# A second level of seven products inside products 1 and 4 of the up layer, three of four pairs of groups, in a routing attention followed by a squared-ReLU layer

## The chip, the core and the metric

The kernel runs on one core of a Trainium2 chip. The core has a matrix engine (TensorE, PE in the profile; its weight loads are PEld), a vector engine (VectorE, DVE), an engine for activation functions (ScalarE, ACT), a general engine (GpSimd, POOL) and one that mostly issues transfers (SyncE, SP). Each runs its own instructions in order and waits for the others on semaphores. Matmuls write to PSUM[...]; all else lies in SBUF, 128 partitions wide. The metric is the time of one execution on the device in microseconds; less is better.

## The reference

```python
def _attn_ref(q, k, v, centroids):            # B, H, S, D = 4, 8, 768, 64; 16 centroids
    q_assign = np.argmax(np.einsum('bhsd,hcd->bhsc', q_n, c_n), axis=-1)
    k_assign = np.argmax(np.einsum('bhsd,hcd->bhsc', k_n, c_n), axis=-1)
    mask = q_assign[:, :, :, None] == k_assign[:, :, None, :]
    scores = scale * np.matmul(q, k.transpose(0, 1, 3, 2))
    scores = np.where(mask, scores, -1000000000.0)
...
    return np.matmul(attn, v).astype(np.float32)

def _moe_ref(x, w_in, w_out):                 # x 3072x512, w_in 512x2048, w_out 2048x512
    h = x @ w_in
    r = np.maximum(h, 0.0)
    g = r * r
    return (g @ w_out).astype(np.float32)
```

The attention's output, turned to 3072 rows of 512, is the x of the second part. The change touches only `h = x @ w_in` and the square.

## The kernel before

**Stages.** The attention runs first, up to about 320 us. Then the four batches follow each other in the order of FEED, 1, 2, 3, 0; each has an up stage (h and its square) and a down stage (times w_out). The first batch (n = 0) has code of its own, `first_up` and `first_down`. The others (n = 1, 2, 3) run `up` and then `Down.run`. Everything from n = 1 on has its order written out by hand: an engine runs its instructions in the order in which the program issues them.

**An up stage.** All matrices are stored with the contracted dimension on the partitions. w_in is 4 x 128 rows by 2048 columns, x of a batch 4 x 128 rows by 768 columns. Each up stage splits all three matrices in two by two and uses Strassen's scheme with seven products in place of eight (the variant of Winograd). The loop `for i in range(F2)` goes over eight groups; a group makes four blocks of 128 x 384: c11 and c12 (row block i, the two halves of the columns) and c21 and c22 (row block 8 + i). A product is two matmuls of 128 x 384 in one bank (L790). `group` (L780) names the operands: products 1, 2 and 4 use w_in as it is, products 3, 5, 6 and 7 use sums of w_in blocks (`w_sums`, L566, four instructions on GpSimd for each group, into one of two buffers taken in turn); products 4 to 7 use sums of x, made once for a batch by `x_sums` (x_t1, x_t2, x_t4). `combine` (L733) issues the products in the order 1, 6, 2, 7, 5, 4, 3. ScalarE copies product 1 from its bank to c11, and VectorE adds or subtracts each of the others from its bank (L747 and L551).

**Behind these additions**, in `up`: `square` (L765) puts two ScalarE instructions on a finished block, the maximum with 0 and the square. `first_level` (L954) adds three VectorE instructions on the group before, the sums that the down stage's own first level needs, into `home`. `third_sums` (L966) adds four more and stores them to DRAM for the rows that two batches share. `behind_seven` in the last group is `Down.parts`, the operand sums of the first unit of the down stage. The last block of the last group is squared by VectorE (L770).

**A down stage** applies seven products twice, one inside the other: it runs 14 or 7 units of seven products, each product four matmuls of 128 columns (L979). Of the right operands, sums of w_out were stored to DRAM (`w_far`) in `first_down`; `load_right(j)` (L936) loads four of them, 256 KB each, over SP's queue into the four `slot`s, which are the upper 1024 columns of the two `home` tiles. Before the change `Down.__init__` loads those of j = 1 before the up stage begins, so that they lie in the slots while it runs.

**Banks.** PSUM is split into a pool `banks` of six and a pool `lows` of two, which only the rounding of the weights in `first_up` uses. A bank is given out again after the last reader of what was in it six allocations ago.

Of the kernel before, what the change touches and what calls it, by code (L numbers as in the profile page):

```python
# [8 lines left out]
F32 = mybir.dt.float32  # L9
# [16 lines left out]
def kernel(  # L26
# [688 lines left out]
    lows = fast.enter_context(tc.tile_pool(name="lows", bufs=2, space=PSUM, reuse_waits="tile"))  # L715
# [64 lines left out]
    def group(i, g, sums_of_w, sums_of_x):  # L780
        a, s1, s2, s3, s4 = sums_of_w
        x, t1, t2, t3, t4 = sums_of_x
        operands = {
            1: (a[0][0], x[0][0]), 2: (a[0][1], x[1][0]), 3: (s4, x[1][1]), 4: (a[1][1], t4),
            5: (s1, t1), 6: (s2, t2), 7: (s3, t3),
        }

        def product(j, bank):
            for kk in range(H2):
                nc.tensor.matmul(  # L790
                    bank, lhsT=operands[j][0][:, kk], rhs=operands[j][1][:, kk],
                    start=(kk == 0), stop=(kk == H2 - 1),
                )

        return [[g[:, f, h] for h in range(2)] for f in (i, F2 + i)], product

    def first_up(b, g, rounding):
# [20 lines left out]
            rounding.behind(i)  # L818
        xT.pop(b)

    def up(b, g, n, x, behind_seven):
        for i in range(F2):
            c, product = group(i, g, w_sums(i, n == B - 1), x)

            def behind_add(j):
                if j == 6 and i:
                    first_level(g, i - 1)
                elif j == 2:
                    square(c[0][0])
                    if i:  # L830
                        third_sums(g, n, i - 1)()
                elif j == 7 and i == F2 - 1:
                    behind_seven()
                elif j == 5:
                    square(c[1][1])

            combine(c, product, TB, behind_add=behind_add)
            square(c[1][0])
            (square if i < F2 - 1 else square_by_dve)(c[0][1])
        xT.pop(b)  # L840

    last_w_sum = [None]
# [145 lines left out]
    class Down:  # L988
        def __init__(self, b, g, n):
            self.b, self.g, self.n = b, g, n  # L990
            both = n % 2
            self.units = (
                [(0, 1), (0, 4), (1, 4), (1, 1)] if both else [(0, 1), (0, 4)]
            ) + [(of, j) for j in RIGHT_ORDER[2:] for of in range(1 + both)]
            load_right(1)
            a = blocks(g, TWO)
            s1, s2 = (s_home(i) for i in range(2))
            self.lefts = {
                1: a[0][0], 2: a[0][1], 3: s1, 4: a[1][1], 5: s1, 6: s2, 7: a[1][0]
            }  # L1000
            self.a, self.s1, self.s2 = a, s1, s2
            self.count = 0
            self.stores = []
# [188 lines left out]
    class Rounding:  # L1192
# [68 lines left out]
    for n, b in enumerate(FEED):  # L1261
        g = gp.tile([P, FT, 2, TB], F32, name="g")
        if n == 0:
            first_up(b, g, Rounding())
            first_down(b, g)
            again = nc.values_load(flag[0:1, 0:1], min_val=0, max_val=1)
            with tc.issue_after(last_w_sum[0]):
                sum_x(1, 4)
            manual.enter_context(
                tc.manual_schedule(engines={E.PE, E.DVE, E.Activation, E.Pool, E.SP})  # L1270
            )
# [196 lines left out]
```

## Time and profile before

| | us |
|---|---|
| median of 3 runs | 884.16 (883.78 to 885.28) |
| the profiled execution | 884.7 |
| its span, first to last instruction | 882.9 |
| up stage of n = 1, 2, 3, each | 72.24 |
| down stages of n = 1, 2, 3 | 87.5, 43.8, 87.6 |

The profile was taken in one execution. Its page gives busy time of each engine and the chain of work that ended last; the trace behind it can be asked for single instructions. Busy time of one engine in a stretch of one kind can be set against another's there, which a mean over the span can't show: the attention and the six stages of n = 1 to 3 differ in what VectorE, ScalarE and the transfers do. A float32 matmul appears as two records, so a group of 112 matmuls is "x224".

In an up stage a group takes 9.03 us. VectorE has seven additions and subtractions from banks in it (0.55 us each, two of them from product 5's bank), the three of first_level (about 0.42 us each) and the four of third_sums (about 0.28 us each). ScalarE has one copy (0.46 us) and eight halves of squares (0.52 us). GpSimd has four sums (0.72 us).

### The profile page before, as it was taken

What the parts mean: (1) busy time and instruction counts of PE and PEld (TensorE: products, weight loads), DVE (VectorE), ACT (ScalarE), POOL (GpSimd) and SP (SyncE); (2) the same over time, 40 slices, a digit from 0 to 9 for tenths busy, and PEclk for the clock granted to TensorE, in tenths of its full rate; (3) what the DMA queues carried; (4) which work ended last, traced back from release to release, by engine and by line L of the source; (5) the groups of instructions that cost most, each with busy time, mean ns of one, the idle gap of its engine ahead of it and who ended that gap; (6) DMA issues with size and microseconds to landing.
All of it is one profiled execution on the core that took longest, in us unless ns stands there. A gap on an engine that the chain in (4) does not pass through costs nothing.

```text
span 882.9 us, 14581 instructions
## 1 busy us (share of the span) xinstructions
PE 876.2 (99%) x5379; PEld 584.6 (66%) x5379; DVE 703.4 (80%) x1272; ACT 390.0 (44%) x621; POOL 145.8 (17%) x168
## 2 busy tenths in 40 slices
PE   9999999999999999999999999999999999999997
PEld 6444444444444455568855589996557985569997
DVE  6799888888888999999846586797568786676786
ACT  5877667777666657740044510002543014540000
POOL 0000010000010236730132200004320043210000
PEclk9999999999999999999999999999999999999999
DMA  7777897767763335236811156583113751117563
GB/s 252 171 188 197 217 268 176 208 180 201 200 185 99 97 129 182 72 109 226 312 45 49 42 153 191 165 275 101 55 42 103 232 174 42 48 49 243 158 203 123
DMA packets 166401, 136.04 MB, mean 154 GB/s; under 512 B 58826, under 2 KB 140082, under 8 KB 166066
## 3 DMA queue, kind: packets, MB, share of 16 engines
q1 hardware_dynamic: 149938, 119.92, 45.5%
q10 hardware_dynamic: 16384, 15.11, 5.6%
q8 instruction: 45, 0.74, 0.3%
q14 instruction: 34, 0.28, 0.1%
HBM read 82.10 MB, written 41.89 MB: 140 GB/s over the span
## 4 chain that ended last, share of the span: by engine, by line
PE 99%; DMA 0%; ACT 0%; DVE 0%; issue 0%
PE bank L790 33%; PE bank L979 25%; PE sc L441 14%; PE av_a L475 10%; PE bank L871 5%; PE av_b L475 5%; PE sc L450 4%; PE sc L329 1%; PE sc L494 1%; DMA q_raw<-in_q_dram 0%; PE av_a L289 0%; ACT ex L457 0%; PE av_a L274 0%; PE sc L274 0%; PE av_b L274 0%; PE av_b L289 0%
## 5 line engine op out<-in xcount | busy, mean ns | idle before, releaser
L457 ACT ACTIVATE ex<-sc 128x1024 f32<-128x1024 f32 x144 | 144.2, 1025 | 37.5 <-PE sc L441 31.6
L747 DVE TENSOR_TENSOR g<-bank,g 128x384 f32<-128x384 f32 x192 | 102.6, 553 | 72.9 <-PE bank L790 67.5
L441 PE MATMUL sc<-qkT 64*128 64x512 f32 (+1 forms) x768 | 150.5, 484 | 0.0
L766 ACT ACTIVATE g<-g 128x384 f32<-128x384 f32 x122 | 63.5, 520 | 104.3 <-DVE g L747 100.1
L441 PEld LDWEIGHTS sc<-qkT 64*128 64x128 f32 x768 | 65.6, 188 | 42.1 <-issue 30.2
L790 PE MATMUL bank<-xT,w_in 128*128 128x384 f32 x256 | 93.2, 487 | 0.0
L790 PE MATMUL bank<-xT,w_s 128*128 128x384 f32 x256 | 93.1, 486 | 0.0
L790 PE MATMUL bank<-x_t,w_s 128*128 128x384 f32 x256 | 93.0, 486 | 0.0
L1131 ACT COPY spare<-bank 128x128 f32<-128x128 f32 x35 | 9.2, 264 | 189.7 <-PE bank L979 165.7
L475 PE MATMUL av_a<-ex,v_raw 128*64 128x512 f32 x384 | 85.9, 596 | 0.0
L460 DVE TENSOR_TENSOR total<-total,ex 128x1024 f32<-128x1024 f32 x64 | 78.7, 1229 | 6.5
L571 POOL TENSOR_TENSOR w_s<-w_in 128x256 f32<-128x256 f32 x32 | 25.5, 797 | 315.4 <-PE bank L979 148.0
L979 PE MATMUL bank<-home,l 128*128 128x128 f32 x560 | 74.0, 275 | 0.0
L790 PEld LDWEIGHTS bank<-xT,w_s 128*128 128x128 f32 x256 | 48.6, 190 | 34.2 <-issue 0.6
L790 PEld LDWEIGHTS bank<-x_t,w_s 128*128 128x128 f32 x256 | 48.6, 190 | 33.9
L790 PEld LDWEIGHTS bank<-xT,w_in 128*128 128x128 f32 x256 | 48.3, 190 | 33.7 <-DVE g L551 0.6
L161 POOL TENSOR_TENSOR w_in<-w_in,w_raw 128x512 int32<-128x512 int32 x16 | 21.4, 1339 | 294.8 <-DVE w_in L153 294.8
L979 PEld LDWEIGHTS bank<-home,l 128*128 128x128 f32 x560 | 68.2, 192 | 0.0
L767 ACT ACTIVATE g<-g 128x384 f32<-128x384 f32 x122 | 63.8, 523 | 3.9
L475 PEld LDWEIGHTS av_a<-ex,v_raw 128*64 128x64 f32 x384 | 26.2, 137 | 51.0 <-issue 49.3
L450 PE MATMUL sc<-rows 64*128 64x512 bf16 (+1 forms) x360 | 58.8, 323 | 0.0
L790 PE MATMUL bank<-x_t,w_in 128*128 128x384 f32 x128 | 46.5, 486 | 0.0
(192 smaller groups left out, 1410.1 us busy)
## 6 DMA issues: line engine op xcount, KB each, us to landing
home<-w_far SPq DMA_DIRECT2D x92, 256.0 KB
words<-flat SPq DMA_DIRECT2D x26, 384.0 KB
w_raw<-in_moe_w_in_dram SPq DMA_DIRECT2D x16, 512.0 KB
w_raw<-in_moe_w_out_dram SPq DMA_DIRECT2D x16, 512.0 KB
w_far<-home SPq DMA_DIRECT2D x28, 256.0 KB
g<-g_far SPq DMA_DIRECT2D x28, 256.0 KB
v_raw<-in_v_dram SPq DMA_DIRECT2D x16, 384.0 KB
g_far<-third SPq DMA_DIRECT2D x24, 256.0 KB
```

Source lines behind the costliest of these rows:

```text
L441: nc.tensor.matmul(sc[i][:, e, cols], lhsT=qkT[pair][rows, NCH + c], rhs=qkT[pair][rows, n.start // P : n.stop // P], start=first, stop=no ...
L450: nc.tensor.matmul(sc[i][:, e, cols], lhsT=ohT[pair][rows, 1, c * P : (c + 1) * P], rhs=ohT[pair][rows, 0, columns(i)], start=first, stop= ...
L457: nc.scalar.activation(out=ex[i], in_=sc.pop(i), func=ACT.Exp, scale=SCALE)
L460: eng.tensor_tensor(out=out, in0=a, in1=b, op=ALU.add)
L475: nc.tensor.matmul(bank[D * e : D * (e + 1), 0 : n.stop - n.start], lhsT=raw_v[pair][:, e, c], rhs=ex[i][:, e, cols], start=c == 0, stop=c ...
L571: nc.gpsimd.tensor_tensor(out=s1, in0=a[1][0], in1=a[1][1], op=ALU.add)
L747: nc.vector.tensor_tensor(out=out, in0=bank, in1=to, op=ALU.add)
L766: nc.scalar.activation(out=to, in_=to, func=ACT.Relu)
L767: nc.scalar.square(to, to)
L790: nc.tensor.matmul(bank, lhsT=operands[j][0][:, kk], rhs=operands[j][1][:, kk], start=(kk == 0), stop=(kk == H2 - 1),)
L871: nc.tensor.matmul(bank, lhsT=left[j][:, f], rhs=right(j)[:, f], start=(f == 0), stop=(f == F2 - 1),)
L979: nc.tensor.matmul(bank, lhsT=left[:, f], rhs=rhs[:, f], start=(f == 0), stop=(f == F4 - 1))
```

## The change

Two groups together have a product 1 with a left operand of two blocks by two (two groups, two blocks of the contracted dimension) and a right operand of two by two (the same two blocks, two halves of 192 columns). The change does this product, and product 4 in the same way, with a second level of seven products of 128 x 192, one matmul each, in place of eight. Product 4 of groups 0 and 1, 2 and 3, 4 and 5 goes there, and product 1 of groups 2 and 3, 4 and 5, 6 and 7; product 1 of groups 0 and 1, and product 4 of groups 6 and 7 stay as they were.

- `second_lefts` makes the four sums of w_in blocks (128 x 128) on GpSimd. They lie in the last 256 columns of each home tile, one set for both products.
- `second_rights` makes four sums of 128 x 192 on VectorE, once a stage for each of the two products, also in the homes' upper columns.
- `second` issues the seven matmuls: the first alone, which ScalarE copies from its bank, then six; VectorE then adds from the banks in four instructions. Two of the banks come from `banks`, the first product's and one more come from a new pool `more`, which takes the place of `lows` after `first_up`.
- Product 1's result is written to c11 of both groups; product 4's result is written to `spare` and subtracted from c21 of both groups by one instruction of 768 elements.
- The order in `up` changes: an even group issues products 6, 2, 7, 5, 3, an odd one 6, 7, then product 4's first matmul, 5, product 4's other six, the first of product 1 for the next two groups, 2, 3. The other six of product 1 open the next even group. The squares of c21 and the steps first_level and third_sums follow when both groups of a pair are done; group 6 therefore has two of each, for groups 4 and 5.
- `w_sums` of the next group is issued at the start of a group, ahead of the new sums on GpSimd.
- `load_right(1)` moves from `Down.__init__` to group 6 of the up stage, since the new sums use the slots before.

```diff
+    QT = TB // 2
+
+    def second_lefts(j, i):
+        first, k = (0, 0) if j == 1 else (F2, H2)
+        a = [
+            [w_in[:, k + kk, P * f : P * (f + 1)] for kk in range(2)]
+            for f in (first + i, first + i + 1)
+        ]
+        s1, s2, s3, s4 = (
+            home[2 * (m // 2)][:, F2 * PAIR + 4 * QT :][:, P * (m % 2) : P * (m % 2 + 1)]
+            for m in range(4)
+        )
+        nc.gpsimd.tensor_tensor(out=s1, in0=a[1][0], in1=a[1][1], op=ALU.add)
+        sub(s2, s1, a[0][0], nc.gpsimd)
+        sub(s3, a[0][0], a[1][0], nc.gpsimd)
+        sub(s4, a[0][1], s2, nc.gpsimd)
+        return a, s1, s2, s3, s4
+
+    def second_rights(j, right):
+        b = [[right[:, kk, QT * t : QT * (t + 1)] for t in range(2)] for kk in range(2)]
+        t1, t2, t3, t4 = (
+            home[0 if j == 1 else 2][:, F2 * PAIR + QT * m : F2 * PAIR + QT * (m + 1)]
+            for m in range(4)
+        )
+        sub(t1, b[0][1], b[0][0])
+        sub(t2, b[1][1], t1)
+        sub(t3, b[1][1], b[0][1])
+        sub(t4, b[1][0], t2)
+        return b, t1, t2, t3, t4
+
+    def second(lefts, rights, flat, first, step):
+        a, s1, s2, s3, s4 = lefts
+        b, t1, t2, t3, t4 = rights
+
+        def two_of(bank):
+            return bank.rearrange("p (i n) -> p i n", i=2)
+
+        rows = flat[:, first : first + 2 * step].rearrange("p (i n) -> p i n", n=step)
+        top, third, right_two = rows[:, 0, 0 : 2 * QT], rows[:, 1, 0:QT], rows[:, :, QT : 2 * QT]
+        middle = flat[:, first + QT : first + QT + 2 * (step - QT)].rearrange(
+            "p (i n) -> p i n", n=step - QT
+        )[:, :, 0:QT]
+        fourth = rows[:, 1, QT : 2 * QT]
+        one = more.tile([P, QT], F32, name="more", tag="more")
+        nc.tensor.matmul(one, lhsT=a[0][0], rhs=b[0][0], start=True, stop=True)
+        nc.scalar.copy(out=fourth, in_=one)
+        yield
+        c26, c75 = (two_of(bank_tile(2 * QT)) for _ in range(2))
+        c34 = two_of(more.tile([P, 2 * QT], F32, name="more", tag="more"))
+        for bank, left, right in (
+            (c26[:, 0], a[0][1], b[1][0]), (c26[:, 1], s2, t2),
+            (c75[:, 0], s3, t3), (c75[:, 1], s1, t1), (c34[:, 1], a[1][1], t4),
+            (c34[:, 0], s4, b[1][1]),
+        ):
+            nc.tensor.matmul(bank, lhsT=left, rhs=right, start=True, stop=True)
+        plus(two_of(top), c26, fourth.unsqueeze(1).to_broadcast([P, 2, QT]))
+        plus(third, c75[:, 0], rows[:, 0, QT : 2 * QT])
+        plus(right_two, c75[:, 1].unsqueeze(1).to_broadcast([P, 2, QT]), middle)
+        plus(middle, c34, middle)
+        yield
+
     def up(b, g, n, x, behind_seven):
...
         for i in range(F2):
-            c, product = group(i, g, w_sums(i, n == B - 1), x)
...
+            w, w_next = w_next, w_sums(i + 1, odd) if i + 1 < F2 else None
+            ((c11, c12), (c21, c22)), product = group(i, g, w, x)
+            ends, late = i >= F2 - 2, i % 2
...
+            if i < 2:
+                nc.scalar.copy(out=c11, in_=result(1))
+            elif not late:
+                next(unit_1)
+                if ends:
+                    load_right(1)
+            if not (late or ends):
+                lefts[4] = second_lefts(4, i)
+            add(6, (c12, c11))
+            levels_1()
+            if i == 1:
+                rights[1] = second_rights(1, x[0][0][0])
+            if not late or ends:
+                two()
+            if i == 0:
+                rights[4] = second_rights(4, x[4])
+            add(7, (c21, c12))
+            if i == F2 - 1:
+                behind_seven()
+            elif ends:
+                levels_1()
+            r = spare_tile.rearrange("p i n -> p (i n)")
+            if late and not ends:
+                unit_4 = second(lefts.pop(4), rights[4], r, 0, TB)
+                next(unit_4)
+            add(5, (c22, c21), (c12, c12))
+            square(c22)
+            if i == F2 - 2:
+                levels_2()
+            if ends:
+                sub(c21, c21, result(4))
+            elif late:
+                next(unit_4)
+                unit_1 = second(
+                    second_lefts(1, i + 1), rights[1], flat, 2 * TB * (i + 1), 2 * TB
+                )
+                next(unit_1)
+                both = g[:, F2 + i - 1 : F2 + i + 1, 0]
+                sub(both, both, r.rearrange("p (i n) -> p i n", i=2))
+                for k in range(2):
+                    square(both[:, k])
+                two()
+            add(3, (c12, c12))
+            if ends:
+                square(c21)
+            (square if i < F2 - 1 else square_by_dve)(c12)
+            done.extend([i] if ends else [i - 1, i] if late else [])
...
-            load_right(1)
...
+                low_banks.close()
...
+            more = fast.enter_context(
+                tc.tile_pool(name="more", bufs=2, space=PSUM, reuse_waits="tile")
+            )
```

Here `levels_1` is first_level of the oldest group that is done, `levels_2` its third_sums, and `two` is product 2, its addition, the square of c11 and `levels_2`.

More of the change, by code (lines that the diff above doesn't have):

```diff
@@ L714 @@
     banks = fast.enter_context(tc.tile_pool(name="banks", bufs=6, space=PSUM, reuse_waits="tile"))
-    lows = fast.enter_context(tc.tile_pool(name="lows", bufs=2, space=PSUM, reuse_waits="tile"))
+    low_banks = ExitStack()
+    lows = low_banks.enter_context(
+        tc.tile_pool(name="lows", bufs=2, space=PSUM, reuse_waits="tile")
+    )
     outp = fast.enter_context(tc.tile_pool(name="outp", bufs=2, reuse_waits="tile"))
@@ L821, in up @@
     def up(b, g, n, x, behind_seven):
+        flat = g.rearrange("p f h n -> p (f h n)")
+        odd = n == B - 1
+        w_next = w_sums(0, odd)
+        lefts, rights, done = {}, {}, []
         for i in range(F2):
-            c, product = group(i, g, w_sums(i, n == B - 1), x)
[L825 to L835, printed above, removed]
@@ L837, in up, with result, add @@
-            combine(c, product, TB, behind_add=behind_add)
-            square(c[1][0])
-            (square if i < F2 - 1 else square_by_dve)(c[0][1])
+            w, w_next = w_next, w_sums(i + 1, odd) if i + 1 < F2 else None
+            ((c11, c12), (c21, c22)), product = group(i, g, w, x)
+            ends, late = i >= F2 - 2, i % 2
+            def result(j):
+                bank = bank_tile(TB)
+                product(j, bank)
+                return bank
+            def add(j, *results):
+                bank = result(j)
+                for out, to in results:
+                    plus(out, bank, to)
@@ new lines, in levels_1, with levels_2, two @@
+            def levels_1():
+                if done:
+                    first_level(g, done[0])
+            def levels_2():
+                if done:
+                    third_sums(g, n, done.pop(0))()
+            def two():
+                add(2, (c11, c11))
+                square(c11)
+                levels_2()
[5 more added lines that the diff above has]
+                    load_right(1)
@@ new lines, in up @@
+            if late and not ends:
[4 more added lines that the diff above has]
+            if i == F2 - 2:
+                levels_2()
+            if ends:
[11 more added lines that the diff above has]
+                two()
@@ L1270 @@
                 tc.manual_schedule(engines={E.PE, E.DVE, E.Activation, E.Pool, E.SP})
+            )
+            more = fast.enter_context(
+                tc.tile_pool(name="more", bufs=2, space=PSUM, reuse_waits="tile")
             )
```

## The prediction

> **What bounds the kernel now.** I read the page first, then the chain of waits in order of time, then busy time by stretches of the three up stages that change, and last the timelines of VectorE and GpSimd where a stage hands over to the next. The page says that TensorE is never idle and that the chain is nothing but matmuls:
>
> ```profile
> PE   876.2 (99%) x5379; PEld 584.6 (66%) x5379; DVE 703.4 (80%) x1272; ACT 390.0 (44%) x621; POOL 145.8 (17%) x168
> PE 99%; DMA 0%; ACT 0%; DVE 0%; issue 0%
> PE bank L790 33%; PE bank L979 25%; PE sc L441 14%; PE av_a L475 10%; PE bank L871 5%; PE av_b L475 5%; PE sc L450 4%; PE sc L329 1%; PE sc L494 1%; DMA q_raw<-in_q_dram 0%; PE av_a L289 0%; ACT ex L457 0%; PE av_a L274 0%; PE sc L274 0%; PE av_b L274 0%; PE av_b L289 0%
> ```
>
> So the end moves only if TensorE gets less to do, or starts to wait. The chain in order of time (start, length, engine, tile, line, records) gives the price of a matmul, since these stretches have no gap in them; a float32 matmul is two records:
>
> ```profile
> 393.48 24.17 PE bank L871 x112
> 442.14 72.24 PE bank L790 x224
> 514.38 87.54 PE bank L979 x784
> ```
>
> An up stage (L790) has 112 matmuls of 384 columns: 72.24/112 = 645.0 ns each. Of 256 columns: 24.17/56 = 431.6 ns. Of 128 columns: 87.54/392 = 223.3 ns. The three lie on a line. Per stretch (length, then busy time of PE, PEld, DVE, ACT, POOL), the second half of the first changed up stage and the down stage after it:
>
> ```profile
> 478.26:496.30 18.04, 18.04 (x58) 10.62 (x57) 11.23 (x28) 9.07 (x19) 5.65 (x8) 1.00 0.12 44
> 496.30:514.38 18.08, 18.08 (x59) 10.66 (x58) 12.41 (x31) 7.80 (x16) 2.83 (x4) 1.00 0.12 44
> 514.38:601.93 87.55, 87.55 (x786) 87.55 (x785) 70.33 (x136) 5.23 (x18) 5.41 (x6) 1.00 0.68 205
> ```
>
> VectorE has 5.7 to 6.8 us in 18 to spare there. The stretches 601.93 to 674.17 and 717.94 to 790.18 read the same.
>
> [...] one 128x768 subtraction, 0.95 us alone, took 1.48 us beside GpSimd, and GpSimd's 0.72 us became 1.44:
>
> ```profile
> 718.36 1.48 DVE L551 TENSOR_TENSOR xT<-xT 128x768 f32<-128x768 f32 x1
> ...
> 718.98 1.44 POOL L551 TENSOR_TENSOR w_s<-w_in 128x256 f32<-128x256 f32 x1
> ```
>
> **The change part by part.**
>
> *TensorE, removed and added.* A pair of groups does product 1 (or 4) with 2 groups x 2 matmuls x 645.0 = 2580 ns. A unit of the second level does it with seven matmuls of 192 columns. No row shows 192 columns. Halfway between 128 and 256 is 327.5 ns[...]. I take 328[...]. A unit is 7 x 328 = 2296 ns: 284 ns saved[...]. Product 1 changes for groups 2 to 7, product 4 for groups 0 to 5: six units a stage, three stages, 18 units. 18 x 0.284 = 5.1 us (4.9 to 5.5). All of it is on the chain.
>
> *VectorE, which must keep up.* Prices from the timelines, issue to issue: an addition from a bank 0.47 us (0.55 if the next depends on it), the three of first_level 1.12, the four of third_sums 0.93, the three of parts 1.93. A 192-column one lies between 0.28 (128) and 0.41 (256): 0.35. A unit adds three instructions of 384 elements and one of 192, each dependent on the one before: about 1.95 us. Per stage: + 6 x 1.95 for the units, + 3 x 0.96 for the subtraction of 768 elements, + 8 x 0.30 for second_rights, - 6 x 0.55 for the old subtractions of product 4 = + 13.7 us. Before it had 9.29 + 11.23 + 11.23 + 12.41 = 44.2; after 57.9 of 72.24 - 1.70 = 70.5 us, 82%. Taken pair by pair, groups 2 and 3 give VectorE 14.6 us in TensorE's 17.5, and where GpSimd overlaps first_level, second_rights or the 768-element subtraction, up to about 1.5 more by the contention seen above. So it lags by half a microsecond within a pair and catches up in the next. TensorE has six banks and two of the pool "more" ahead of it, several microseconds. Cost: nothing.
>
> *The hand-over to the down stage.* This is the tightest place. In the page's run the end of the first up stage looks like this:
>
> ```profile
> 511.51 0.68 DVE L856 TENSOR_TENSOR l<-g 128x512 f32<-128x512 f32 x1
> ...
> 514.83 0.55 DVE L747 TENSOR_TENSOR g<-bank,g 128x384 f32<-128x384 f32 x1
> 515.42 0.56 DVE L770 SCALAR_TENSOR_TENSOR g<-g 128x384 f32<-128x384 f32 x1
> 516.08 0.42 DVE L856 TENSOR_TENSOR home<-g 128x256 f32<-128x256 f32 x1
> ...
> 517.40 0.69 DVE L551 TENSOR_TENSOR g<-g,l 128x512 f32<-128x512 f32 x1
> ```
>
> The last is the subtraction that feeds the seventh product of the first down unit, 6 x 0.893 us after TensorE leaves the up stage (514.22 + 5.36 = 519.58). It ends at 518.09, so 1.5 us are free. After: count from TensorE's start of group 6, which takes it 6 x 0.328 + 6 x 1.29 = 9.71 us; group 7 takes 6 x 1.29 = 7.74; the down stage starts at 17.45. Group 6 gets two first_level and two third_sums, because a pair is released late. VectorE: unit until 3.05, addition of product 6 at 3.53 (0.27 us after TensorE ends it, as in before), first_level to 5.13, product 2 to 5.60, third_sums to 6.53, product 7, first_level to 8.12, product 5 to 9.05, third_sums to 9.98, product 4, product 3 from 10.45 to 11.0. ScalarE then squares two blocks (0.56 + 0.43 + 0.56 + 0.52) and ends at 12.64; first_level of group 6 waits for that. From there VectorE is back to back: to 13.78, product 2, third_sums to 15.18, product 7 to 15.65, parts to 17.58, products 5, 4, 3 at 18.97, and 2.57 us later, as between 514.83 and 517.40 above, the subtraction: 21.54 to 22.23. It is needed at 17.45 + 5.36 = 22.81. So the lag grows by 0.9 us and 0.4 to 0.6 us stay free: cost nothing, at worst 1 us a stage if VectorE is slower than these prices. The next unit has 1.7 us, since the operands of its third product are ready at 23.6 and wanted at 25.5.
>
> *GpSimd.* second_lefts has one set of four homes for both products. Each unit's left sums can begin only when the unit before has left TensorE, and GpSimd runs them behind w_sums of the next group. Its price: 0.72 us for 256 columns[...]. In an odd group TensorE leaves unit 4 at 14.6 us of the pair[...]; TensorE meanwhile has 0.33 + 2 x 1.29 us, and wants s2 at 17.8 and s4 at 19.1. w_sums of the next group ended at 11.6.[...] In the other direction half a pair is free. Cost nothing.
>
> *ScalarE.* Six copies of 384 (0.46 us) become six of 192: a little less. The first copy of a unit stands behind the squares of product 5's block and ends 2 us before VectorE wants it.
>
> *SP and DMA.* load_right(1), four loads of 256 KB, moves from before the up stage into group 6. It waits there for unit 1 to leave its homes (2 us into the group) and stands ahead of the stores of third_sums in SP's queue. Issue took 3.0 us for four; landing is wanted 15 us later. The stores of groups 4 and 5 come after 6.5 us, so nothing is held. Before the first changed stage the homes must be free of the stores to w_far, the last issued at about 436; the old loads behind them began at 436.6, so the stores are done by 447, when the sums are wanted.
>
> Sum: 884.7 (the profiled execution's time; its span is 882.9) - 5.1 = 879.6. The median of the runs shown is 884.16, 0.5 below that execution: 884.16 - 5.1 = **879.1 us**.
>
> **The rivals.**
> *A. The hand-over takes part of it.* If the unit's additions cost 2.3 instead of 1.95 us, or ScalarE's squares come later, the subtraction misses its 0.5 us and TensorE waits 0.3 to 1 us in each of three stages: 880 to 882. For: VectorE is at nearly 100% in groups 6 and 7. Against: the count leaves room.
> *B. It nets to nothing.* If 192 columns cost as much as a seventh of the old product (369 ns), or VectorE needs over 17.5 us a pair, the saving is gone: 884. Against: the straight line through three widths; 2.9 us of room in each pair.
> *C. Slower.* The single set of homes serializes GpSimd and TensorE. If a left sum takes over 1.0 us, s4 misses 19.1 us in a pair. The contended instructions above took 1.44 us with 256 columns. It decides from 1.25 us a sum: the four end at 14.85 + 5.0 = 19.85, TensorE waits 0.75 us in each of nine pairs, 6.8 us, and the saving of 5.1 is lost with 1.7 on top: 886. At 1.4 us a sum the wait is 1.35, in all 12.2: 891. Against: 128 columns are half the work, and the instructions of VectorE then running mostly read a bank.
>
> **How the numbers follow.** Forecast 0.73, A 0.12, B 0.07, C 0.08. What the runs of this kernel can tell from no change is about 0.2%, 1.8 us: below 882.4 is faster. The forecast and A are faster, B the same, C slower: 0.85, 0.07, 0.08. The forecast's own range is 878.4 to 880.0 (5.5 saved; 4.9 saved and a small wait). To hold eight in ten it takes in A: 878.2 to 882.0.
>
> **What would show it.** Right: the changed up stages last 70.5 us each in the chain, of TensorE alone; 192-column matmuls follow each other by 328 ns; VectorE at about 82% there; the down stages keep 87.5 and 43.8 us. Wrong: idle time of TensorE before the seventh product of a first down unit, released by VectorE (A); idle time at a unit's second or last matmul, released by GpSimd (C); or a longer 192-column matmul (B).

## The result and the profile after

| | before | after |
|---|---|---|
| first comparison, median (lowest to highest) | 884.41 us (883.62 to 886.74) | 881.49 us (881.06 to 882.29) |
| ratio, 95% interval | | 0.9965 [0.9952, 0.9978] |
| second comparison, at another time | 884.14 us (883.16 to 884.89) | 881.86 us (880.75 to 882.64) |
| ratio, 95% interval | | 0.9973 [0.9963, 0.9984] |
| span of the profiled execution | 882.9 us | 880.5 us |
| up stages | 72.24 each | 70.41 each |
| down stages | 87.54, 43.77, 87.71 | 88.58, 44.65, 88.58 |

A stage is taken from its first matmul to the first of the next stage, the last down stage to the end of its last matmul.

The change makes the kernel faster, by some 2.3 to 2.9 us where 5.1 were forecast. The forecast of 879.1 is missed by 2.4 us; 881.5 lies inside the range and is what rival A gives. The last two rows say where the difference is: the three up stages gave 5.48 us, the three down stages, whose code the change doesn't touch but for one moved load, took 2.80 back.

Busy time of each engine, and the chain of work that ended last by engine and line, from the page of the changed kernel:

```profile
PE 871.7 (99%) x5487; PEld 600.3 (68%) x5487; DVE 753.9 (86%) x1359; ACT 385.9 (44%) x621; POOL 181.2 (21%) x240
PE 76%; DVE 18%; ACT 2%; issue 2%; DMA 2%; DVEq 0%; ACTq 0%; SPq 0%
PE bank L1109 22%; PE bank L793 14%; PE sc L441 13%; PE av_a L475 9%; DVE g L986 7%; PE bank L1001 6%; PE av_b L475 4%; PE sc L450 3%; DVE third L551 2%; DVE g L551 2%; DVE spare L986 2%; DVE home L551 2%; PE sc L329 1%; DVE home L986 1%; PE sc L494 1%
```

TensorE is still busy for 99% of the span, but the chain, which was TensorE to 99%, runs through VectorE for 18%. That is not 18% of VectorE's time to be saved: one wait of TensorE is enough to send the chain back through the work of VectorE in front of it (that of 0.6 us which ends at 518.62 sends it back to 470.02). It says that somewhere TensorE now waits for VectorE.

By stretches of the changed kernel (length, then busy time of PE, PEld, DVE, ACT, POOL), the first up stage, its down stage, the second down stage and the third up stage:

```profile
442.07:512.48 70.41, 70.41 (x261) 47.10 (x260) 58.60 (x132) 32.00 (x66) 30.86 (x52) 1.00 0.16 55
512.48:601.06 88.58, 87.97 (x785) 87.69 (x784) 72.38 (x140) 5.58 (x18) 5.08 (x6) 1.00 0.66 201
...
671.48:716.13 44.65, 44.03 (x393) 43.84 (x392) 39.41 (x73) 3.73 (x11) 5.17 (x6) 1.00 0.65 205
716.13:786.54 70.41, 70.41 (x262) 47.11 (x261) 63.53 (x139) 31.79 (x66) 33.25 (x51) 1.00 0.18 59
```

The up stages have no idle time of TensorE (70.41 of 70.41). The down stages have 0.6 us each (88.58 against 87.97). The waits of TensorE from the first changed up stage on (microseconds in all, number, longest):

```profile
PE bank L1109 <- DVE g L551: 1.8, 3, 0.6
```

and where it lies, in TensorE's order of time at the first hand-over (start, length, line, records, idle time before it and who ended it):

```profile
512.48 1.95 PE L1109 MATMUL bank<-w_out,g 128*128 128x128 f32 x16
...
516.95 1.06 PE L1109 MATMUL bank<-home,g 128*128 128x128 f32 x8
518.62 1.16 PE L1109 MATMUL bank<-w_out,g 128*128 128x128 f32 x8 [0.61 <-DVE g L551]
```

The three waits are one and the same: the seventh product of the first down unit, which waits for VectorE's subtraction. Without a wait it starts 5.36 us after the stage (512.48 + 5.36 = 517.84, as 519.58 against 514.22 in the kernel before). It starts at 518.62, so 0.78 us are lost, and the product then takes 1.16 instead of 1.06: a wait of 0.61 costs 0.88. Three of these are 2.64 of the 2.80 us. The other 0.16 is at one product in the thirteenth unit of the first down stage, at 590.27 us: two of its matmul records start 0.19 us after the one before instead of 0.11. The trace names no cause there. The gated kernel below waits in the same unit, for the load of a slot, so that is the likely one.

The price of a 192-column matmul, from TensorE's order of time in the first unit of product 4:

```profile
455.30 0.49 PE L883 MATMUL bank<-x_t,w_in 128*128 128x192 f32 x2
455.62 1.14 PE L883 MATMUL bank<-home 128*128 128x192 f32 x6
456.60 0.49 PE L883 MATMUL more<-home,w_in 128*128 128x192 f32 x2
456.93 0.49 PE L883 MATMUL more<-x_t,home 128*128 128x192 f32 x2
457.25 0.49 PE L873 MATMUL more<-xT,w_in 128*128 128x192 f32 x2
```

From 455.30 to 457.25 there are six (two records each): 325 ns each. A unit saves 2580 - 7 x 325 = 305 ns, 18 of them 5.5 us.

What VectorE and GpSimd did before that wait, from the timeline of the changed kernel. TensorE begins group 6 at 495.06; the four `third` lines are third_sums at the end of group 5, `g<-more` is the last addition of the unit that opens group 6, the last line is the subtraction that TensorE waits for:

```profile
495.12 0.28 DVE L986 TENSOR_TENSOR third<-g 128x128 f32<-128x128 f32 x1
495.43 0.74 DVE L551 TENSOR_TENSOR third<-third,g 128x128 f32<-128x128 f32 x1
496.10 0.28 DVE L551 TENSOR_TENSOR third<-g 128x128 f32<-128x128 f32 x1
496.30 0.81 DVE L551 TENSOR_TENSOR third<-g,third 128x128 f32<-128x128 f32 x1
...
499.20 0.56 DVE L986 TENSOR_TENSOR g<-more,g 128x384 f32<-128x384 f32 x1
...
508.98 0.43 DVE L986 TENSOR_TENSOR home<-g 128x256 f32<-128x256 f32 x1 [1.18 <-ACT g L770]
...
517.87 0.69 DVE L551 TENSOR_TENSOR g<-g,l 128x512 f32<-128x512 f32 x1
...
495.30 0.72 POOL L571 TENSOR_TENSOR w_s<-w_in 128x256 f32<-128x256 f32 x1 [1.74 <-PE bank L793]
496.10 0.86 POOL L551 TENSOR_TENSOR w_s<-w_s,w_in 128x256 f32<-128x256 f32 x1
496.93 0.78 POOL L551 TENSOR_TENSOR w_s<-w_in 128x256 f32<-128x256 f32 x1
```

GpSimd's sums for group 7 fall on VectorE's third_sums. Two of the four sums take 0.74 and 0.81 us instead of 0.29, and the four take 1.92 (495.12 to 497.04, the issue of VectorE's next instruction) instead of 0.93. The unit is done 4.70 us after TensorE's start of group 6, where the prediction has 3.05, and the subtraction ends 23.50 after it, where 22.8 was the limit. That suggests a theory: the overlap in group 6 makes the wait.

### The profile page after: what moved, and what is told of

Read it like the earlier page. It is cut to its first block, busy times and chain, and to the rows that moved or that the text cites. A ratio compares the mean times of both kernels' runs of the same rounds, so it can differ in the third digit from the quotient of the medians.

```text
span 880.5 us, 14989 instructions
## 1 busy us (share of the span) xinstructions
PE 871.7 (99%) x5487; PEld 600.3 (68%) x5487; DVE 753.9 (86%) x1359; ACT 385.9 (44%) x621; POOL 181.2 (21%) x240
## 4 chain that ended last, share of the span: by engine, by line
PE 76%; DVE 18%; ACT 2%; issue 2%; DMA 2%; DVEq 0%; ACTq 0%; SPq 0%
PE bank L1109 22%; PE bank L793 14%; PE sc L441 13%; PE av_a L475 9%; DVE g L986 7%; PE bank L1001 6%; PE av_b L475 4%; PE sc L450 3%; DVE third L551 2%; DVE g L551 2%; DVE spare L986 2%; DVE home L551 2%; PE sc L329 1%; DVE home L986 1%; PE sc L494 1%
## 5 line engine op out<-in xcount | busy, mean ns | idle before, releaser
L986 DVE TENSOR_TENSOR g<-bank,g 128x384 f32<-128x384 f32 (+3 forms) x205 | 102.2, 514 | 19.8 <-PE bank L793 11.8
L793 PE MATMUL bank<-xT,w_in 128*128 128x384 f32 x184 | 67.1, 487 | 0.0
L793 PEld LDWEIGHTS bank<-xT,w_in 128*128 128x128 f32 x184 | 34.4, 190 | 21.7 <-DVE g L551 0.6
L1109 PE MATMUL bank<-home,g 128*128 128x128 f32 x352 | 46.5, 275 | 0.0
```

The costliest lines, as they stand in the source:

```text
L793: nc.tensor.matmul(bank, lhsT=operands[j][0][:, kk], rhs=operands[j][1][:, kk], start=(kk == 0), stop=(kk == H2 - 1),)
L986: nc.vector.tensor_tensor(out=out, in0=one, in1=two, op=ALU.add)
L1109: nc.tensor.matmul(bank, lhsT=left[:, f], rhs=rhs[:, f], start=(f == 0), stop=(f == F4 - 1))
```

## The experiments

### Take the overlap away: e1 and e2

The first holds GpSimd back until third_sums is through, with a sum of one column that reads its last result (`last_third` keeps that tile); this is called the gate from here on. The second leaves the sums for group 7 out in the three up stages. Group 7 then computes with those of group 6, so that version only shows what the sums cost.

```diff
+            if i == F2 - 2:
+                nc.gpsimd.tensor_tensor(
+                    out=gate, in0=last_third[0][:, 3, 0:1], in1=last_third[0][:, 3, 0:1], op=ALU.add
+                )
             w, w_next = w_next, w_sums(i + 1, odd) if i + 1 < F2 else None
```

> In group 6 GpSimd first adds one column of the last third_sums to itself, so that w_sums of group 7 starts only when that third_sums has ended. Theory 1 (GpSimd's sums of group 7 stretch the third_sums that stands ahead of group 6 from 0.93 to 1.9 us, group 6 is too full to take the lag back, and it arrives at the hand-over): third_sums about 0.95 us, the subtraction of the first down unit 0.6 to 1.0 us earlier after the start of group 6, TensorE's wait there falls from 0.61 to 0.0 to 0.2 us a stage, span 878.0 to 879.0. Theory 2 (the two first_level and two third_sums of group 6 and the squares behind them set the lag by themselves): the wait stays at 0.4 to 0.6 us a stage, span 880.2 to 880.6.

```diff
-            w, w_next = w_next, w_sums(i + 1, odd) if i + 1 < F2 else None
+            w, w_next = w_next, w if i == F2 - 2 else w_sums(i + 1, odd) if i + 1 < F2 else None
```

> Left out: the sums of w_in for group 7 in the last three up stages; group 7 uses those of group 6. GpSimd has nothing to do in groups 6 and 7. Theory 1: the third_sums ahead of group 6 takes 0.93 us, the wait of TensorE at the hand-over is 0.0 to 0.1 us a stage, down stages 87.6, 43.8 and 87.7 us, span 877.8 to 878.3. Theory 2: the wait stays at 0.4 to 0.6 us a stage, span 880.2 to 880.6.

Measured beside 884.21 us of the kernel before: the gate 879.32 us (878.86 to 880.40), ratio 0.9947 [0.9930, 0.9964]; without the sums 878.5 us (877.72 to 879.33), ratio 0.9934 [0.9917, 0.9951]. Neither has a wait at the hand-over. The timeline of the gated kernel, VectorE, GpSimd's gate and TensorE's seventh product:

```profile
494.35 0.28 DVE L992 TENSOR_TENSOR third<-g 128x128 f32<-128x128 f32 x1
494.67 0.29 DVE L551 TENSOR_TENSOR third<-third,g 128x128 f32<-128x128 f32 x1
494.88 0.28 DVE L551 TENSOR_TENSOR third<-g 128x128 f32<-128x128 f32 x1
495.08 0.29 DVE L551 TENSOR_TENSOR third<-g,third 128x128 f32<-128x128 f32 x1
...
516.13 0.69 DVE L551 TENSOR_TENSOR g<-g,l 128x512 f32<-128x512 f32 x1
...
495.44 0.19 POOL L897 TENSOR_TENSOR gate<-third 128x1 f32<-128x1 f32 x1 [2.67 <-DVE third L551]
...
517.04 1.06 PE L1116 MATMUL bank<-w_out,g 128*128 128x128 f32 x8
```

All four sums are at 0.28 to 0.29 again, and the subtraction ends at 516.82, 0.22 us before TensorE wants it. The subtraction comes 0.93 us earlier, more than the 0.72 by which it was late. So in the changed kernel the overlap is needed for the wait. Whether it is enough by itself, these two don't say.

### Move third_sums of group 6 into the down stage: e3

```diff
                 square(c11)
-                levels_2()
+                if i < F2 - 1:
+                    levels_2()
...
                 if u == 0:
+                    third_sums(self.g, self.n, F2 - 2)()
                     store = third_sums(self.g, self.n, F2 - 1)
```

> third_sums of group 6 (four instructions of VectorE, 0.93 us) moves from group 7 to the first down unit, behind the subtraction and the next operand sums. Both theories of the lag say that the subtraction comes 0.93 us earlier and is about in time: wait 0.0 to 0.1 us a stage, span 877.9 to 878.5. If the wait were for something else than VectorE's queue (a transfer, a square), it stays: span 880.5.

885.25 us (883.79 to 886.96), ratio 1.0013 [1.0004, 1.0022]: neither expectation was met. From its timeline, TensorE at the hand-over and in the fourth unit of that stage, and VectorE's first operand sum of the first down unit:

```profile
517.22 1.16 PE L1110 MATMUL bank<-w_out,g 128*128 128x128 f32 x8 [0.53 <-DVE g L551]
...
534.29 1.13 PE L1110 MATMUL bank<-home,l 128*128 128x128 f32 x8 [1.62 <-DMA home<-w_far]
...
510.57 0.69 DVE L987 TENSOR_TENSOR l<-g 128x512 f32<-128x512 f32 x1 [0.75 <-ACT g L770]
```

VectorE had 0.93 us less to do in group 7, but then waited 0.75 us for ScalarE's square of c11, which third_sums had covered: 0.18 us gained. And the moved stores stand ahead of the loads of the next slots in SP's queue: the second load of slots in the down stage begins to issue at 529.47 instead of 528.74, although this stage starts 1.3 us earlier, so 2.0 us later in the stage, and TensorE waits 1.62 us for a slot. (The third down stage has another wait, of 0.83 us for VectorE.) So this step, which looked free to move, paid through ScalarE on one side (0.75 us) and through SP's queue on the other (1.62 us).

### Product 2 ahead of first_level in group 7: e4 and f_gate_two

In the changed kernel VectorE waits 1.18 us for ScalarE in group 7 (the line at 508.98) with product 2's addition behind it. This puts that addition first:

```diff
             add(6, (c12, c11))
+            if i == F2 - 1:
+                add(2, (c11, c11))
+                square(c11)
             levels_1()
...
-            if not late or ends:
+            if i == F2 - 1:
+                levels_2()
+            elif not late or ends:
                 two()
```

> In group 7 the addition of product 2 goes ahead of first_level of group 6, into the 1.18 us in which VectorE waits for ScalarE's squares. If that wait is a part of the lag, all that follows comes 0.47 us earlier and TensorE's wait falls from 0.61 to 0.1 to 0.3 us a stage: span 879.0 to 879.6. If the wait for ScalarE moves with it (the squares come later, or product 2 is late), span 880.3 to 880.6.

880.3 us (879.39 to 881.44), ratio 0.9957 [0.9941, 0.9974]; the wait at the hand-over falls from 0.61 to 0.24 us in the first stage and 0.16 in the other two, and VectorE's idle time from 1.18 to 0.52. That is the first reading of the two. Later, the gate alone, the gate with this edit and the changed kernel again on one chip, beside 884.14 of the kernel before:

> The changed kernel again, beside the versions that remove its wait, on one chip. Theory 1 (the contention of w_sums with third_sums in group 6 makes TensorE wait 0.6 us three times): as before, ratio 0.9965 +- 0.001, three waits of 0.6 us before the seventh product of the first down unit.

> The version in which GpSimd starts the sums for group 7 only behind the third_sums of the last pair but one, beside the changed kernel on one chip. Theory 1: 2.0 to 2.8 us less than the changed kernel, ratio to before 0.994; all of the 5.5 us of TensorE is kept. Rival (the wait is only where VectorE's lag shows, and lifting it there moves it elsewhere): within 1 us of the changed kernel.

> The gate of GpSimd and, in group 7, product 2's addition ahead of first_level of group 6. Theory 1: the gate already takes the whole wait away, so the second edit adds nothing that can be measured: the same as with the gate alone to 0.5 us. Rival (some of the lag is left, in waits of under 0.1 us all over the hand-over): up to 1 us less than with the gate alone.

| | us | ratio to before | span less start of the first changed up stage |
|---|---|---|---|
| before | 884.14 (883.16 to 884.89) | | 440.9 |
| changed | 881.86 (880.75 to 882.64) | 0.9973 [0.9963, 0.9984] | 438.5 |
| gate | 880.03 (879.39 to 882.17) | 0.9959 [0.9945, 0.9973] | 436.4 |
| gate and product 2 first | 880.43 (878.71 to 881.02) | 0.9956 [0.9943, 0.9970] | 435.9 |

The last column is from the profiled executions (for the kernel before, that of the first comparison). It is there because the first changed stage starts 440.8 to 442.4 us into the span, from execution to execution.

The three waits of the changed kernel are there again, and absent in the other two. By its median the gate brings 1.8 us over the changed kernel here, just under what was expected; by its trace 2.1. In that trace it loses 0.7 us again in the first down stage (88.26 us against 87.54 before), most of it where TensorE waits for a slot's load:

```profile
589.81 1.13 PE L1116 MATMUL bank<-home 128*128 128x128 f32 x8 [0.31 <-DMA home<-w_far]
```

The two gated kernels can't be told apart by time. The second edit moves the subtraction only from 22.5 to 22.1 us after the start of group 6, where 22.8 is enough, so the gate had already removed the wait. The gated kernel is faster than the kernel before in both of its comparisons. That it is faster than the changed kernel rests on the medians and the traces, since the intervals of the second comparison overlap.

### One product alone

If the wait comes from a group 6 that is too full, half the change may bring as much as the whole. First product 4 alone, with product 1 as in the kernel before:

```diff
-            if i < 2:
-                nc.scalar.copy(out=c11, in_=result(1))
-            elif not late:
-                next(unit_1)
-                if ends:
-                    load_right(1)
+            nc.scalar.copy(out=c11, in_=result(1))
+            if i == F2 - 2:
+                load_right(1)
...
-                unit_1 = second(
-                    second_lefts(1, i + 1), rights[1], flat, 2 * TB * (i + 1), 2 * TB
-                )
-                next(unit_1)
```

> Only product 4 goes to the second level, product 1 stays as it was in every group (9 units in place of 18; group 6 has no unit of product 1 at its start, so VectorE is 1.8 us earlier there, and group 6 and 7 take TensorE 0.3 us more). Theory 1 with its second half (group 6 is too full to take the contention's 1 us back): no wait at the hand-over, up stages of 71.3 us, saving 9 x 0.305 = 2.7 us, ratio 0.997, which is as much as both products bring in the changed kernel. Rival (the contention alone makes the wait, however full group 6 is): the three waits stay at 0.6 us, 0.9 with the restart, and the time is that of before, ratio 1.000.

887.84 us (886.95 to 888.11), ratio 1.0040 [1.0027, 1.0054]: slower than before, and slower than either theory expected. From its timeline, VectorE and ScalarE at the start of group 6, and TensorE's seventh product:

```profile
497.75 0.54 DVE L977 TENSOR_TENSOR g<-bank,g 128x384 f32<-128x384 f32 x1
499.80 0.56 DVE L977 TENSOR_TENSOR g<-bank,g 128x384 f32<-128x384 f32 x1 [1.51 <-ACT g L923]
...
498.88 0.52 ACT L770 ACTIVATE g<-g 128x384 f32<-128x384 f32 x1
499.31 0.46 ACT L923 COPY g<-bank 128x384 f32<-128x384 f32 x1
...
519.38 1.16 PE L1100 MATMUL bank<-w_out,g 128*128 128x128 f32 x8 [0.72 <-DVE g L551]
```

There is a new wait. ScalarE copies product 1 in its own order behind the squares of the pair before, which hang on VectorE's last addition (497.75). VectorE's first addition of the next group needs that copy. The two engines wait for each other in turn, 1.5 us in group 6 and 2.0 in group 7. In the first stage the subtraction is then 1.5 us late. TensorE waits twice in each first down unit: 0.36 us for a copy by ScalarE and 0.72 for the subtraction. The changed kernel has a copy at this place too, but of the unit's first matmul, ahead of the squares. Two kernels tell the overlap and this copy apart: the gate on GpSimd, and the last squares of a group put behind the copy of the next:

```diff
             nc.scalar.copy(out=c11, in_=result(1))
+            for to in later:
+                square(to)
+            later = []
...
-            if ends:
-                square(c21)
-            (square if i < F2 - 1 else square_by_dve)(c12)
+            later = ([c21] if ends else []) + [c12]
+            if i == F2 - 1:
+                square(c21)
+                square_by_dve(c12)
```

> Only product 4, with GpSimd's sums for group 7 held until third_sums is done. Reading A (the waits of the version with product 4 alone come from the overlap, 3.06 us for four sums of third_sums that take 1.1 alone): the waits of 0.7 us go or fall under 0.2, about 882, ratio 0.998. Reading B (they come from VectorE waiting 1.5 and 2.0 us for ScalarE's copy of product 1, which stands behind the squares of the group before): waits stay at 0.5 us or more, ratio 1.002 to 1.004.

> Only product 4, with ScalarE's copy of product 1 ahead of the last squares of the group before. Reading A: the overlap still costs VectorE 2 us, so the waits fall by half at most, ratio 1.002. Reading B: VectorE no longer waits for the copy and has 3 us more, no wait at the hand-over, 881.5, ratio 0.997.

Beside 884.05 of the kernel before: with the gate 889.51 us (889.15 to 890.12), ratio 1.0060 [1.0043, 1.0077], more than either reading had, and the wait at the seventh product still 0.72; with the copy ahead 882.0 us (880.37 to 882.34), ratio 0.9973 [0.9962, 0.9984], and no wait. VectorE in the version with the copy ahead, whose group 6 begins at 494.02:

```profile
494.59 0.70 DVE L551 TENSOR_TENSOR third<-third,g 128x128 f32<-128x128 f32 x1
...
495.42 0.81 DVE L551 TENSOR_TENSOR third<-g,third 128x128 f32<-128x128 f32 x1
...
515.88 0.69 DVE L551 TENSOR_TENSOR g<-g,l 128x512 f32<-128x512 f32 x1
```

The overlap is still there: the four sums take 1.88 us, as in the changed kernel. Yet the subtraction ends 0.86 us before it is wanted. So Reading B holds for this version: there the copy decides, and the overlap alone makes no wait. The gated version says less. It frees third_sums in group 6, but two earlier ones, which the gate doesn't reach, took 3.07 and 1.52 us in its execution, so VectorE came late all the same.

Then product 1 alone, with the pairwise release of first_level and third_sums, and with one release for each group:

```diff
-            if not (late or ends):
-                lefts[4] = second_lefts(4, i)
...
-            if ends:
-                sub(c21, c21, result(4))
-            elif late:
-                next(unit_4)
+            sub(c21, c21, result(4))
+            if late and not ends:
                 unit_1 = second(
...
-                both = g[:, F2 + i - 1 : F2 + i + 1, 0]
-                sub(both, both, r.rearrange("p (i n) -> p i n", i=2))
-                for k in range(2):
-                    square(both[:, k])
                 two()
             add(3, (c12, c12))
-            if ends:
-                square(c21)
+            square(c21)
```

and, for the second, `done.append(i)` as its last line.

> Only product 1 goes to the second level, product 4 is as it was (9 units). Groups 6 and 7 and the release by pairs are those of the changed kernel. Theory 1 (the wait comes from group 6, with the unit at its start, two of each step and GpSimd's sums beside them): the hand-over waits of 0.6 us stay, so 2.7 us saved, 2.65 given back, ratio 1.000. Rival (the lag that the units of product 4 leave at the end of group 5 is needed for it): no wait, 881.4, ratio 0.997.

> Only product 1, and first_level and third_sums follow each group, as in the kernel before, so that group 6 has one of each. Theory 1: no wait at the hand-over, up stages of 71.3 us, 2.7 us saved, ratio 0.997. Rival (the unit of product 1 at the start of group 6 is enough for the wait): waits of 0.3 us or more in three stages, ratio 0.999 to 1.000.

881.91 us (880.88 to 883.24), ratio 0.9974 [0.9965, 0.9982], and 882.28 us (881.08 to 882.79), ratio 0.9973 [0.9962, 0.9985]. Neither has a wait at the hand-over. The first is the rival's number: Theory 1 as I had put it, with all of the cause inside group 6, falls. From its timeline, VectorE around the start of group 6, and TensorE's first 192-column matmul of group 6 and seventh product:

```profile
493.76 0.56 DVE L971 TENSOR_TENSOR g<-bank,g 128x384 f32<-128x384 f32 x1 [0.71 <-PE bank L793]
494.24 0.28 DVE L971 TENSOR_TENSOR third<-g 128x128 f32<-128x128 f32 x1
...
494.96 0.28 DVE L551 TENSOR_TENSOR third<-g,third 128x128 f32<-128x128 f32 x1
...
497.49 0.56 DVE L971 TENSOR_TENSOR g<-more,g 128x384 f32<-128x384 f32 x1
...
516.31 0.69 DVE L551 TENSOR_TENSOR g<-g,l 128x512 f32<-128x512 f32 x1
...
494.85 0.49 PE L883 MATMUL bank<-xT,w_in 128*128 128x192 f32 x2
...
517.64 1.06 PE L1094 MATMUL bank<-w_out,g 128*128 128x128 f32 x8
```

Without product 4's unit in group 5 VectorE is early enough to wait for TensorE (0.71 us). third_sums then starts before TensorE enters group 6, and only its last sum, at its usual 0.28 us, still runs when GpSimd's sums begin, at 495.10. So the overlap is no fixed property of group 6: it is a consequence of VectorE's lag. In the version with one release for each group, group 6 begins at 496.33 and the subtraction is this one:

```profile
516.87 0.69 DVE L551 TENSOR_TENSOR g<-g,l 128x512 f32<-128x512 f32 x1
```

In us from TensorE's start of group 6, in the first stage (third_sums up to the issue of the next instruction):

| | third_sums ends | subtraction ends | wanted | left |
|---|---|---|---|---|
| product 1 alone, one release for each group | 0.31 | 21.23 | 22.79 | 1.56 |
| product 4 alone, copy ahead | 2.13 | 22.56 | 23.42 | 0.86 |
| product 1 alone | 0.32 | 22.15 | 22.79 | 0.64 |
| both, gate | 1.03 | 22.57 | 22.79 | 0.22 |
| both (the change) | 1.98 | 23.50 | 22.78 | -0.72 |

Between product 1 alone and both with the gate, the lag that product 4's units leave is worth 0.4 us at the hand-over. The overlap that it brings is worth 0.9. The release by pairs is worth another 0.9 (21.23 against 22.15): the two versions with product 1 alone take the same time only because both are early enough. In the changed kernel it was not taken away by itself. So the wait of 0.6 us has no single cause. Several things are ahead of one deadline, and the overlap is the one that e1 shows to be enough to remove.

## Why the prediction was right in its range and off in its middle

The measured 881.5 us lies within 878.2 to 882.0, but that range was widened to take in rival A, to which the prediction gave 0.12. The forecast's own range, 878.4 to 880.0, is missed. It was off by two terms of opposite sign: TensorE saved 0.4 us more than forecast, and 2.8 us were lost where it has "Cost: nothing".

- **TensorE's saving: right, at the end of its bounds.** 192 columns were taken at 328 ns; they take 325. The saving is 5.48 us, not 5.1, and all of it shows in the up stages. The bounds of 4.9 and 5.5 us were the author's estimate; no run before the change shows a matmul of 192 columns. The three widths are not quite on a line: that through 256 and 384 columns gives 324.9 at 192, and the 128-column row lies 5 ns above it, which made the halfway value too high.
- **"So it lags by half a microsecond within a pair and catches up in the next. ... Cost: nothing": the step that failed.** Two terms of VectorE's sum were too small, and group 6 has no next pair in which to catch up. A unit's additions were priced at 1.95 us; undisturbed, in the first unit, they take 2.30 (456.44 to the subtraction's start at 458.74). With two units a pair that is 0.7 us more. The overlap with GpSimd was counted for the pair, "up to about 1.5 more", without third_sums among the steps that it can meet, and not at all in the count that starts at group 6, where it costs 0.95.
- **"The hand-over to the down stage ... 0.4 to 0.6 us stay free": right as a count, wrong in its start.** The count lets VectorE enter group 6 on time and has the unit done at 3.05 us. Where VectorE does enter on time, with product 1 alone, the unit is done at 3.20, and the subtraction ends at 22.15 of 22.79, against 22.23 of 22.81 forecast. With the gate the unit is done at 3.76, in the change at 4.70: 0.56 from the lag and 0.94 from the overlap. The subtraction then misses by 0.72 and costs 0.88 a stage with the slower restart; "at worst 1 us" was the right bound and "cost nothing" the wrong value. Rival A named the place, the sign by which to know it, and one of the causes, the unit at 2.3 us. It did not name the overlap. (The 1.7 us given to the next unit are 1.9 by the two figures beside it; nothing hangs on that.)
- **GpSimd: right that no left sum delays TensorE** (most take 0.45 to 0.46 us, up to 1.17, that one beside VectorE's sum of 768 columns at 720.48; TensorE has no wait for GpSimd from 440 us on). The prediction shows 0.72 us for 256 columns; that 128 would be ready in time was the author's estimate. What it missed is the other direction: not what GpSimd's own sums wait for but whom they slow. In the changed kernel five additions from banks, from 485.42 to 488.14, four of them beside GpSimd's sums, start 0.54 us apart; the three from 489.89 to 491.47, beside none, start 0.53 us apart. Of the four sums of third_sums, whose two inputs both lie in SBUF, two go from 0.29 to 0.74 and 0.81 us. What makes the two kinds differ was not shown.
- **ScalarE, SP and the moved load: right.** No wait that the changed kernel's trace names comes from them. But e3 and product 4 alone show how close they are: 2.0 us in SP's queue make TensorE wait 1.62 us, and the order of one copy makes VectorE wait 1.5 and 2.0 us, when something is moved.
- **VectorE's load** was forecast at 57.9 us a stage; it is 58.6, 60.9 and 63.5. The 44.2 us at the base of that sum are those of the first stage; in the kernel before, the second and third have 46.2 and 48.4. They read the same only in their second halves. A mean of 83% to 90% said nothing about the end of the stage.
- **The sum.** 5.48 saved less 2.80 given back is 2.7 us; the two comparisons show 2.9 and 2.3.

What stays open: what the release by pairs alone would give in the changed kernel, and whether the 0.16 us in the first down stage are a slot's load.

## What to carry to other kernels

When an engine has 10 to 17% of slack on average, as VectorE has here, count it at the point where a deadline stands, and carry the lag with which it arrives there into the count: a count that starts at zero is the count of another kernel. A lag is not only itself; it can move instructions into the window of another engine's work, and that overlap can cost more than the lag that led to it (0.9 us against 0.4 here). A deadline that is missed by little, here by 0.72 us, need not have a single cause: the gate, worth 0.93 us, removes the wait, and so does leaving product 4 as it was, or product 1 once ScalarE's copy stands ahead. And an equal time of two versions (881.91 and 882.28 us) does not mean that what sets them apart is worth nothing (0.9 us), since both may be early. When the sum of two good edits runs into such a deadline, either half alone may bring as much as both (here 881.9 us with product 1 and 882.0 with product 4 and the copy ahead, against 881.5 and 881.9), and one instruction that holds back the other engine may be cheaper than less work (the gate, 880.0 us beside 881.9).

## What the hardware showed that was not expected

In these traces the price of the overlap goes with a tenth of a microsecond. In the changed kernel, where GpSimd's first sum starts 0.18 us after VectorE's, only the second and fourth of third_sums' additions are slowed (1.92 us for the four). In the kernel with product 4 alone and the gate, at the third_sums between groups 3 and 4, where the gate does nothing yet, all four are, from its timeline:

```profile
477.31 0.85 DVE L983 TENSOR_TENSOR third<-g 128x128 f32<-128x128 f32 x1
478.19 0.77 DVE L551 TENSOR_TENSOR third<-third,g 128x128 f32<-128x128 f32 x1
478.88 0.83 DVE L551 TENSOR_TENSOR third<-g 128x128 f32<-128x128 f32 x1
479.63 0.82 DVE L551 TENSOR_TENSOR third<-g,third 128x128 f32<-128x128 f32 x1
```

That is 3.07 us (477.31 to 480.38) for what takes 0.93 alone, with GpSimd's sums at 0.73 to 0.79 instead of 0.72 to 0.73. The same place in the same program without the gate, where GpSimd's first sum starts at the same moment as VectorE's (476.91 and 476.92) instead of 0.04 us ahead (477.27 and 477.31), takes 1.88 (476.92 to 478.80). At its third_sums behind group 5, where GpSimd is 0.1 us ahead (494.67 and 494.76), all four are slowed again, to 0.77 to 0.82. That the order decides is read from such cases; no run changed the order alone. The load is shared unequally here: VectorE's 128-column sum nearly triples (0.28 to 0.29 us alone, 0.77 to 0.85 beside GpSimd), GpSimd's 256-column one hardly changes (0.73 to 0.79 at this place). Beside VectorE's 768-column subtraction, which the prediction shows, GpSimd's sum doubled (0.72 to 1.44 us).
